# Weight decoding with its scratch in another place, and combined weights through diagonal weights, ahead of a two-layer loop

## The chip, the cores and the metric

One core of one Trainium2 chip runs the kernel. The metric is the device time of one execution in microseconds. The kernel before took 1108.55 us as the median of three runs (1108.22 to 1109.36).

## What is computed

Agent attention over 12480 tokens of 128 channels and 49 agents, and then two feed-forward layers (128 to 2048 to 128), all in float32; the weights of the layers arrive as float64, 8 bytes each:

```
a2k     = softmax(agents @ k.T * scale)        # 49 x 12480
agent_v = a2k @ v                              # 49 x 128
q2a     = softmax(q @ agents.T * scale)        # 12480 x 49
x       = q2a @ agent_v                        # 12480 x 128
x       = silu(x @ w_in) @ w_out
out     = (h * cos(h)) @ w2_out,  h = x @ w2_in
```

## The kernel before, in words

The kernel never forms x of the attention. It multiplies agent_v with w_in once ("combined weights", 49 rows of 2048) and feeds the probabilities q2a of the tokens straight to the first layer. TensorE works on numbers rounded to its float32r form; to keep precision each operand is held as a high part and the rest, a low part, and a product is taken as high x high, low x high and high x low.

It has two stages. The **first stage**, up to about 130 us, loads and prepares everything, and its order of instructions on each engine is planned ahead of time by a scheduler from dependencies and priorities. The **second stage** is the loop over 25 tiles of tokens with four groups each (lines 589 to 865); its order is written out by hand in a block of manual schedule, and the diff leaves that order as it is. The loop's buffers take the memory of the first stage's buffers, and its PSUM banks those of the first stage, so it waits for them to come free.

In the first stage tokens come in 13 blocks: twelve of 1024 tokens and one of 192. All loads are issued by the SP queue, in order. A loop over the key blocks turns them (T, lines 316 to 328), takes scores and a running maximum (k_scores). Three query steps and six decoding steps are put between. Then a loop of query steps runs: each takes a query block through turning (L323, copied by ScalarE at L327), scores (L337), maximum and difference (L119, L123), exponential (L124), normalising on GpSimd (L133), splitting into a packed tile pk of 128 columns (L145 to L147) and turning back (L156), from where a copy (L161, on ScalarE) writes the probabilities pT. Each of these is one step behind the one before. Beside them the key scores become exponentials (L383, with their sums in zk), are turned (L394, L396) and multiplied with v (L408), summing into pav over all blocks.

**Decoding.** The 8-byte weights come in 16 pieces of 128 x 512, four each of i1 (w_in), o1, i2 and o2. load_piece (L239, L241) loads one into a raw buffer wraw, of which there are three. split_a decodes: ScalarE takes the absolute value of the upper words into m (L260); VectorE shifts it into a (L264), adds the sign from the upper words (L267), takes the exponent into m (L270), and makes the rest r from the lower words and m (L273), the last reader of the raw words. split_b, one step later, finishes it: ScalarE casts a to the high half (L283), GpSimd takes a minus high half into m (L284) and adds r to give the low half (L285). a, r and m have two buffers each. Decoding has a priority 150 instructions below its place in the program.

**Combining.** After the last v block the two halves of pav go into `halves` (L478) with the reduced zk as one more column (L479); a product with `both` adds the halves (L481), then come add, reciprocal and scaling (L483 to L485), and a product with `eye3` (L487), 49 x 256, which lays the agents' rows two and a half times side by side: 128 columns for the main weights, and 19 remaining rows in four bands of 32 for the part kept apart. The result is split into avh and avl (L490, L491). Then twice, each behind a query step, four banks of products with w2h and w2l (L495 to L497):

```
for j, cast in ((0, nc.vector.tensor_copy), (2, nc.scalar.copy)):
    q_step(t)
    combine(j, cast)
    q_step_end(t)
    t += 1
```

In combine, six products give the part apart, cast (L502) and subtracted in four bands (L505) into w3; six more give the main part, which replaces w2h and w2l in place (L511 to L513). The loop's first instruction of TensorE, L610, multiplies with w3 into a PSUM pair, and L622 with w2h.

Of the kernel before, what the change touches and what calls it, by code (L numbers as in the profile page):

```python
# [8 lines left out]
F32 = mybir.dt.float32  # L9
# [26 lines left out]
def agent_attention_moe_moe_kernel(ctx, tc, q, k, v, agents, w_in, w_out, w2_in, w2_out, out):  # L36
    nc = tc.nc
# [21 lines left out]
    eye3 = const.tile([NA, 256], F32, name="eye3")  # L59
# [108 lines left out]
    with ExitStack() as att:  # L168
        raw_p = att.enter_context(tc.tile_pool(name="raw", bufs=NRAW))
        wraw_p = att.enter_context(tc.tile_pool(name="wraw", bufs=3))  # L170
        dec_p = att.enter_context(tc.tile_pool(name="dec", bufs=2))
# [61 lines left out]
        def load_piece():  # L233
# [3 lines left out]
            t = wraw_p.tile([128, 512], I64, tag="w", name="wraw")  # L237
# [9 lines left out]
        def split_a():  # L247
# [7 lines left out]
            hi, lo = (x[:, 4 * j:4 * j + 4, :].rearrange("p c d -> p (c d)") for x in split[nm])  # L255
# [5 lines left out]
            half_split.append((hi, lo, a, r, m))  # L261
# [16 lines left out]
        def split_b():  # L278
            if not half_split:
                return  # L280
            hi, lo, a, r, m = half_split.pop(0)
# [10 lines left out]
        for a in (0, NA, 2 * NA):  # L292
            n = min(NA, 128 - a)
            nc.vector.tensor_copy(out=eye3[:, a:a + n], in_=ident[:NA, :n])
        nc.vector.memset(eye3[:, 128:256], 0.0)
        for a in range(128, 256, 32):
            nc.vector.tensor_copy(out=eye3[:, a:a + REST], in_=ident[:NA, MORE:NA])
# [65 lines left out]
        both = one_p.tile([128, NA], F32, name="both")  # L363
        nc.vector.tensor_tensor(out=both, in0=ident[:, 0:NA], in1=ident[:, 64:64 + NA], op=ALU.add)
# [107 lines left out]
        halves = one_p.tile([128, C + 1], F32, name="halves")  # L472
        nc.gpsimd.memset(halves, 0.0)
        assert not todo and not raws

        avn = ag
        for x in (0, 64):
            nc.vector.tensor_copy(out=halves[x:x + NA, 0:C], in_=pav[x:x + NA])  # L478
        nc.vector.tensor_reduce(out=halves[:, C:C + 1], in_=zk, op=ALU.add, axis=AX.X)  # L479
        pav = banky("y1")[:NA, :C + 1]  # L480
        nc.tensor.matmul(out=pav, lhsT=both, rhs=halves, start=True, stop=True)  # L481
        rz = one_p.tile([NA, 1], F32, name="rz")
        nc.vector.tensor_scalar(out=rz, in0=pav[:, C:C + 1], scalar1=1e-9, scalar2=None, op0=ALU.add)  # L483
        nc.vector.reciprocal(out=rz, in_=rz)
        nc.vector.tensor_scalar(out=avn, in0=pav[:, 0:C], scalar1=rz, scalar2=None, op0=ALU.mult)  # L485
        pn = bank1()[:, :256]
        nc.tensor.matmul(out=pn, lhsT=avn, rhs=eye3, start=True, stop=True)  # L487

        avh, avl = (eT_p.tile([128, 512], F32R, tag="eT", name=nm)[:, :256] for nm in ("avh", "avl"))
        nc.vector.tensor_copy(out=avh, in_=pn)  # L490
# [24 lines left out]
        def combine(j, cast):  # L515
            pair = bank2()
            for x in range(2):
                av_times_w(pair[:, x, :], j + x, True)
            apart(pair, j, cast)
            pair = bank2()  # L520
            for x in range(2):
                av_times_w(pair[:, x, :], j + x, False)
# [347 lines left out]
```

## Time and profile before

| | |
|---|---|
| median of three runs | 1108.55 us |
| profiled execution | 1108.43 us |
| its span, first to last instruction | 1106.6 us |
| TensorE busy | 1074.5 us (97%) |
| VectorE busy | 962.3 us (87%) |
| ScalarE busy | 924.6 us (84%) |
| GpSimd busy | 541.1 us (49%) |
| mean granted clock of TensorE | 0.989 of full |

In the profile PE is TensorE, PEld its loading of weights, DVE VectorE, ACT ScalarE, POOL GpSimd and SP the engine that issues the DMAs. Busy time of PE is that of pipelined matmuls, so 97% is not 97% of its peak. A row of the timeline has the start and the length in us, the engine, the line of the kernel, the operation, the output and input tiles, the shape, the count, and in brackets how long the engine stood idle before it and what released it. Clock is the share of full speed that TensorE was granted: 1.00 is 2.4 GHz, 0.50 is 1.2 GHz, and a value between is a mix of the two over the stretch. The span includes both stages; averages over it hide that the first has other limits than the second.

### The profile page before, as it was taken

The page shows a single profiled execution, that of the slowest core. Times are in us where ns is not written, and L with a number is a line of the kernel's source. Part 1 is how long each engine was busy: PE and PEld are TensorE (multiplying, and loading weights), DVE is VectorE, ACT ScalarE, POOL GpSimd, SP SyncE. Part 2 cuts the span into 40 slices and gives each one's busy share as a digit, 9 for nine tenths or more (in the row PEclk, how much of TensorE's full clock was granted, in tenths as well). Part 3 has the DMA queues.
Part 4 walks back from the last instruction along what each step waited for, and adds up shares of the span by engine and source line. Part 5 has one row for each costly group of instructions (what it writes and reads, how often), then busy time and mean ns, then how long its engine had stood idle before and what let it go on. Part 6 is the DMA issues. An engine that isn't in the chain of part 4 may idle for free.

```text
span 1106.6 us, 14122 instructions
## 1 busy us (share of the span) xinstructions
PE 1074.5 (97%) x5227; PEld 844.5 (76%) x5227; DVE 962.3 (87%) x1023; ACT 924.6 (84%) x1005; POOL 541.1 (49%) x281
## 2 busy tenths in 40 slices
PE   8798799999999999999999999999999999999997
PEld 5597567777777777777777777777777777788996
DVE  5868469999999999999999989999999999989897
ACT  6796698888888888888888888888888888888876
POOL 2668305444455444555444555444554444555455
PEclk9998799999999999999999999999999999999999
DMA  9763000000000000000000000000000000000000
GB/s 345 285 235 139 11 6 6 14 3 15 16 8 9 16 13 4 16 16 1 16 16 11 6 16 15 1 16 16 9 8 16 13 4 15 15 5 10 10 9 16
DMA packets 66221, 38.68 MB, mean 35 GB/s; under 512 B 52523, under 2 KB 57184, under 8 KB 66152
## 3 DMA queue, kind: packets, MB, share of 16 engines
q1 hardware_dynamic: 66152, 37.78, 11.3%
q8 instruction: 41, 0.67, 0.3%
q14 instruction: 28, 0.23, 0.1%
HBM read 27.58 MB, written 6.39 MB: 31 GB/s over the span
## 4 chain that ended last, share of the span: by engine, by line
PE 87%; DVE 4%; ACT 3%; POOL 3%; DMA 2%; issue 1%; SPq 0%; POOLq 0%; DVEq 0%; ACTq 0%
PE y L654 16%; PE y L658 16%; PE y L655 16%; PE h L622 10%; PE h L696 8%; PE h L698 8%; PE h L697 8%; PE h L610 4%; DMA raw<-in_q_dram 1%; DMA wraw<-in_moe_w_in_dram 1%; POOL g2l L755 1%; DVE a L267 1%; ACT xT L327 1%; POOL m L284 1%; PE h L323 1%
## 5 line engine op out<-in xcount | busy, mean ns | idle before, releaser
L755 POOL TENSOR_TENSOR g2l<-g,g2h 128x1024 fp32r<-128x1024 f32 (+2 forms) x200 | 465.5, 2350 | 504.8 <-DVE g1l L645 495.0
L720 DVE SCALAR_TENSOR_TENSOR n<-n,h 128x1024 f32<-128x1024 int32 (+3 forms) x202 | 238.9, 1184 | 65.3 <-ACT n L710 52.1
L710 ACT ACTIVATE n<-h,quarter 128x1024 int32<-128x1024 f32 (+3 forms) x202 | 219.7, 1088 | 89.4 <-PE h L698 89.3
L645 DVE TENSOR_TENSOR g1l<-g,g1h 128x1024 fp32r<-128x1024 f32 (+2 forms) x200 | 239.6, 1198 | 23.4 <-ACT g1h L637 16.2
L737 DVE TENSOR_TENSOR g<-n,h 128x1024 f32<-128x1024 f32 (+3 forms) x202 | 237.9, 1178 | 3.4 <-ACT n L729 0.2
L630 ACT ACTIVATE g<-h 128x1024 f32<-128x1024 f32 (+2 forms) x200 | 199.5, 998 | 37.1 <-PE h L622 37.0
L729 ACT ACTIVATE n<-n,halfpi 128x1024 f32<-128x1024 f32 (+3 forms) x202 | 225.7, 1120 | 0.8 <-DVE n L720 0.8
L637 ACT CAST g1h<-g 128x1024 fp32r<-128x1024 f32 (+2 forms) x200 | 204.8, 1024 | 3.3
L746 DVE CAST g2h<-g 128x1024 fp32r<-128x1024 f32 (+2 forms) x196 | 154.5, 788 | 7.5
L654 PE MATMUL y<-g1h,o1h 128*128 128x512 f32 (+2 forms) x400 | 156.7, 392 | 0.5 <-DVE x2l L683 0.4
L654 PE MATMUL y<-g2h,o2h 128*128 128x512 f32 (+2 forms) x400 | 154.6, 386 | 1.1 <-DVE o L777 0.9
L696 PE MATMUL h<-x2h,i2h 128*128 128x512 f32 (+2 forms) x400 | 154.1, 385 | 1.0 <-DVE g L737 0.9
L655 PE MATMUL y<-g2h,o2l 128*128 128x512 f32 (+2 forms) x400 | 154.4, 386 | 0.0
L655 PE MATMUL y<-g1h,o1l 128*128 128x512 f32 (+2 forms) x400 | 154.2, 386 | 0.0
L698 PE MATMUL h<-x2l,i2h 128*128 128x512 f32 (+2 forms) x400 | 153.7, 384 | 0.0
L697 PE MATMUL h<-x2h,i2l 128*128 128x512 f32 (+2 forms) x400 | 153.7, 384 | 0.0
L622 PE MATMUL h<-pT,w2h 128*128 128x512 f32 (+2 forms) x400 | 134.5, 418 | 0.0
L658 PE MATMUL y<-g2l,o2h 128*128 128x512 f32 (+2 forms) x400 | 122.2, 386 | 1.9 <-POOL g2l L755 1.9
L658 PE MATMUL y<-g1l,o1h 128*128 128x512 f32 (+2 forms) x400 | 121.6, 385 | 0.0
L654 PEld LDWEIGHTS y<-g1h,o1h 128*128 128x128 f32 x400 | 75.5, 189 | 21.9 <-DVE x2l L683 8.3
L622 PEld LDWEIGHTS h<-pT,w2h 128*128 128x128 f32 x400 | 68.1, 190 | 31.4 <-issue 24.4
L658 PEld LDWEIGHTS y<-g2l,o2h 128*128 128x128 f32 x400 | 74.8, 188 | 17.7 <-POOL g2l L755 3.1
(119 smaller groups left out, 1145.9 us busy)
## 6 DMA issues: line engine op xcount, KB each, us to landing
raw<-in_q_dram SPq DMA_DIRECT2D x12, 512.0 KB
vraw<-in_v_dram SPq DMA_DIRECT2D x12, 512.0 KB
raw<-in_k_dram SPq DMA_DIRECT2D x11, 512.0 KB
out_dram<-o SPq DMA_DIRECT2D x88, 64.0 KB
wraw<-in_moe_w_in_dram SPq DMA_DIRECT2D x8, 512.0 KB
wraw<-in_moe_w_out_dram SPq DMA_DIRECT2D x8, 512.0 KB
x<-pT SPq DMA_DIRECT2D x88, 38.0 KB
raw<-in_k_dram SPq DMA_DIRECT2D x2, 256.0 KB
```

Source lines behind the costliest of these rows:

```text
L622: nc.tensor.matmul(out=h1s[g, k][:, j, :toks(t)], lhsT=w2h[:, 128 * c:128 * c + 128], rhs=x, start=False, stop=True)
L645: i = v.tensor_tensor(out=gl, in0=f, in1=b32(gh), op=ALU.subtract)
L654: nc.tensor.matmul(out=y, lhsT=wh[:, c, :], rhs=gh[:, j, :], start=(c == 0), stop=False)
L655: nc.tensor.matmul(out=y, lhsT=wl[:, c, :], rhs=gh[:, j, :], start=False, stop=False)
L658: nc.tensor.matmul(out=y, lhsT=wh[:, c, :], rhs=gl[:, j, :], start=False, stop=(c == NCH - 1))
L696: nc.tensor.matmul(out=y, lhsT=i2h[:, c, :], rhs=xh, start=True, stop=False)
L697: nc.tensor.matmul(out=y, lhsT=i2l[:, c, :], rhs=xh, start=False, stop=False)
L698: nc.tensor.matmul(out=y, lhsT=i2h[:, c, :], rhs=xl, start=False, stop=True)
L720: v.scalar_tensor_tensor(out=b32(n)[:, p], in0=n[:, p], scalar=-2.0 * PI, in1=h2s[g, k][:, p], op0=ALU.mult, op1=ALU.add)
L729: sc.activation(out=r[:, p], in_=r[:, p], func=AF.Sin, bias=halfpi)
L737: v.tensor_tensor(out=f[:, p], in0=r[:, p], in1=h[:, p], op=ALU.mult)
L755: i = (v if (g, k) == (NG - 1, 1) else gp).tensor_tensor(out=gl[:, p], in0=f[:, p], in1=b32(gh)[:, p], op=ALU.subtract)
```

## The change

There are two parts. In the **decoding** the raw words of o1, i2 and o2 are loaded into the very place that the two halves will take, and only i1 still uses raw buffers, two in place of three. m comes from a pool of its own, with two buffers, and is no longer written by GpSimd; the difference goes into a. a and r have three buffers. The high half of a piece now overwrites its raw words, so it is written after r has read them. In the **combining** the sum of zk goes through a product of its own, its reciprocal scales the diagonal `eye3` (now 128 x 160), one product with the unscaled `halves` gives what two gave, and the part apart is made by twelve products into one bank, with stationary tiles `spread` that are zero outside 32 columns. Both rounds of combining stand behind one query step. In combine itself only the six products per pair, the in-place casts and the subtraction remain.

```diff
-    eye3 = const.tile([NA, 256], F32, name="eye3")
+    eye3 = const.tile([128, 160], F32, name="eye3")
...
-    split = {"i1": tuple(x.rearrange("p (c d) -> p c d", d=128) for x in (w2h, w2l))}
-    for nm in ("o1", "i2", "o2"):
-        split[nm] = (
-            wts.tile([128, NCH, 128], F32R, name=f"{nm}h"),
-            wts.tile([128, NCH, 128], F32R, name=f"{nm}l"),
-        )
+    parted = {}
+
+    def halves_of(nm, j):
+
+        if nm == "i1":
+            return [x[:, 512 * j:512 * j + 512] for x in (w2h, w2l)]
+        parted[nm, j] = wts.tile([128, 2, 512], F32R, tag=f"{nm}{j}", name=nm)
+        return [parted[nm, j][:, x, :] for x in range(2)]
+
+    def part(nm, x, c):
+        return parted[nm, c // 4][:, x, c % 4 * 128:c % 4 * 128 + 128]
...
-        wraw_p = att.enter_context(tc.tile_pool(name="wraw", bufs=3))
-        dec_p = att.enter_context(tc.tile_pool(name="dec", bufs=2))
+        wraw_p = att.enter_context(tc.tile_pool(name="wraw", bufs=2))
+        dec_p = att.enter_context(tc.tile_pool(name="dec", bufs=3))
+        mag_p = att.enter_context(tc.tile_pool(name="mag", bufs=2))
...
             nm, j = to_load.pop(0)
-            t = wraw_p.tile([128, 512], I64, tag="w", name="wraw")
+            if nm == "i1":
+                t = wraw_p.tile([128, 512], I64, tag="w", name="wraw")
+            else:
+                t = wts.tile([128, 512], I64, tag=f"{nm}{j}", name="wraw")
...
-            m = dec_p.tile([128, 512], F32, tag="m", name="m")
+            m = mag_p.tile([128, 512], F32, tag="m", name="m")
...
+            nm, j, a, r = half_split.pop(0)
+            hi, lo = halves_of(nm, j)
+            f = a.bitcast(F32)
             with tc.high_priority(offset=-LATER):
-                nc.scalar.copy(out=hi, in_=a.bitcast(F32))
-                nc.gpsimd.tensor_tensor(out=m, in0=a.bitcast(F32), in1=b32(hi), op=ALU.subtract)
-                nc.gpsimd.tensor_tensor(out=lo, in0=r, in1=m, op=ALU.add)
+                nc.scalar.copy(out=hi, in_=f)
+                nc.gpsimd.tensor_tensor(out=f, in0=f, in1=b32(hi), op=ALU.subtract)
+                nc.gpsimd.tensor_tensor(out=lo, in0=r, in1=f, op=ALU.add)
...
+        nc.vector.memset(eye3, 0.0)
+        for x in (0, 64):
+            for a in (0, NA, 2 * NA):
+                n = min(NA, 128 - a)
+                nc.vector.tensor_copy(out=eye3[x:x + NA, a:a + n], in_=ident[x:x + NA, x:x + n])
+            nc.vector.tensor_copy(out=eye3[x:x + NA, 128:128 + REST], in_=ident[x:x + NA, x + MORE:x + NA])
...
-        both = one_p.tile([128, NA], F32, name="both")
-        nc.vector.tensor_tensor(out=both, in0=ident[:, 0:NA], in1=ident[:, 64:64 + NA], op=ALU.add)
+        both = one_p.tile([128, 128], F32, name="both")
+        for x in (0, 64):
+            nc.vector.tensor_tensor(out=both[:, x:x + 64], in0=ident[:, 0:64], in1=ident[:, 64:128], op=ALU.add)
...
+        spread = [v_p.tile([128, 640], F32R, tag="v", name="spread") for _ in range(2)]
+        for x in spread:
+            nc.gpsimd.memset(b32(x), 0.0)
+        halves = one_p.tile([128, C], F32, name="halves")
         nc.gpsimd.memset(halves, 0.0)
...
+        rz = one_p.tile([128, 1], F32, name="rz")
+        nc.vector.tensor_reduce(out=rz, in_=zk, op=ALU.add, axis=AX.X)
+        pz = bank1()[:, 0:1]
+        nc.tensor.matmul(out=pz, lhsT=both, rhs=rz, start=True, stop=True)
+        nc.vector.tensor_scalar(out=rz, in0=pz, scalar1=1e-9, scalar2=None, op0=ALU.add)
         nc.vector.reciprocal(out=rz, in_=rz)
...
+        nc.vector.tensor_scalar(out=eye3, in0=eye3, scalar1=rz, scalar2=None, op0=ALU.mult)
+        nc.vector.tensor_copy(out=halves[0:NA], in_=pav[0:NA])
+        nc.scalar.copy(out=halves[64:64 + NA], in_=pav[64:64 + NA])
+        pn = bank1()[:, :160]
+        nc.tensor.matmul(out=pn, lhsT=halves, rhs=eye3, start=True, stop=True)
+
+        avh, avl = (eT_p.tile([128, 512], F32R, tag="eT", name=nm)[:, :128] for nm in ("avh", "avl"))
+        spread_h, spread_l = (x.rearrange("p (i d) -> p i d", d=160)[:, :, 0:32] for x in spread)
+        four = pn[:, 128:160].unsqueeze(1).to_broadcast([128, 4, 32])
+        nc.scalar.copy(out=avh, in_=pn[:, 0:128])
+        nc.scalar.copy(out=spread_h, in_=four)
+        nc.vector.tensor_tensor(out=avl, in0=pn[:, 0:128], in1=b32(avh), op=ALU.subtract)
+        nc.vector.tensor_tensor(out=spread_l, in0=four, in1=b32(spread_h), op=ALU.subtract)
+
+        def combine_apart():
+
+            pw = banky("y1")
+            y = pw.rearrange("p (c d) -> p c d", c=4)
+            wh, wl = (w.rearrange("p (c i d) -> p c i d", i=4, d=128) for w in (w2h, w2l))
             for i in range(4):
+                for x, w in ((0, wh), (0, wl), (1, wh)):
+                    nc.tensor.matmul(
+                        out=y, lhsT=spread[x][:, 128 * i:128 * i + 128], rhs=w[:, :, i, :],
+                        start=(i == 0 and w is wh and x == 0), stop=(i == 3 and x == 1),
+                    )
+            hr = eT_p.tile([128, 512], F32R, tag="eT", name="hr")
+            nc.scalar.copy(out=hr, in_=pw)
+            nc.vector.tensor_tensor(
+                out=w3.rearrange("p c d -> p (c d)"), in0=pw, in1=b32(hr), op=ALU.subtract
+            )
...
-        for j, cast in ((0, nc.vector.tensor_copy), (2, nc.scalar.copy)):
-            q_step(t)
-            combine(j, cast)
-            q_step_end(t)
-            t += 1
+        q_step(t)
+        combine_apart()
+        combine(0, nc.scalar.copy)
+        combine(2, nc.vector.tensor_copy)
+        q_step_end(t)
+        t += 1
```

The rest of the diff renames what the loop reads: `part(nm, x, c)` in place of the two whole tiles.

## Rows read from the trace of the kernel before

**Rows 1.** Windows by stage: us, each engine busy (x instructions), clock, DMA share, GB/s.

```profile
8.00:41.00 33.00, 28.79 (x185) 17.17 (x183) 23.31 (x37) 27.04 (x39) 12.58 (x11) 1.00 0.89 332
...
55.00:85.00 30.00, 28.73 (x308) 26.76 (x309) 18.09 (x33) 29.22 (x61) 20.81 (x22) 1.00 0.69 241
...
85.00:106.00 21.00, 16.32 (x152) 14.66 (x150) 18.56 (x26) 12.16 (x23) 16.14 (x15) 0.84 0.42 151
...
106.00:131.00 25.00, 17.80 (x87) 13.73 (x86) 16.22 (x34) 13.79 (x23) 13.42 (x16) 0.84 0.04 13
...
131.00:141.00 10.00, 10.00 (x30) 6.79 (x31) 3.34 (x3) 8.67 (x10) 0.00 (x0) 0.55 0.01 2
```

**Rows 2.** Timeline, 98 to 102 us: start, us, engine, line, tiles, count, [idle before].

```profile
98.84 0.67 ACT L260 ACTIVATE m<-wraw 128x512 f32<-128x512 f32 x1 [3.83 <-POOL o2l L285]
...
100.36 0.57 ACT L161 CAST pT<-y 128x512 fp32r<-128x512 f32 x1
...
101.07 1.08 PE L156 MATMUL y<-ident,pk 128*128 128x128 f32 x4 [4.18 <-ACT pT L161]
```

**Rows 3.** Windows, finer, around the gap on TensorE.

```profile
97.00:101.00 4.00, 0.00 (x0) 0.00 (x0) 3.04 (x6) 2.16 (x6) 2.26 (x3) 0.76 0.34 118
...
101.00:106.00 5.00, 4.93 (x24) 4.48 (x24) 4.30 (x7) 2.42 (x5) 4.20 (x4) 0.50 0.01 3
...
106.00:119.00 13.00, 11.22 (x64) 9.17 (x62) 9.43 (x24) 7.20 (x15) 12.23 (x13) 0.87 0.06 19
```

**Rows 4.** Timeline, 105 to 131 us: from the last L408 to the first L610.

```profile
105.45 0.67 PE L408 MATMUL y<-vraw,eT 96*49 96x128 f32 x4
...
106.95 0.29 DVE L478 COPY halves<-y 49x128 f32<-49x128 f32 x1
...
110.56 0.42 PE L481 MATMUL y<-halves,both 128*49 128x129 f32 x2
...
113.39 0.33 DVE L485 TENSOR_SCALAR ag<-y,rz 49x128 f32<-49x128 f32 x1
...
114.16 0.70 PE L487 MATMUL h<-eye,ag 49*128 49x256 f32 x2
...
114.90 0.42 DVE L490 CAST avh<-h 128x256 fp32r<-128x256 f32 x1 [0.46 <-PE h L487]
...
115.45 0.48 PE L495 MATMUL h<-w2h,avh 128*128 128x512 f32 x1
...
118.09 0.39 PE L497 MATMUL h<-w2h,avl 128*128 128x512 f32 x1
...
126.67 1.11 ACT L511 ACTIVATE w2l<-h,from 32x1024 fp32r<-32x1024 f32 x1 [1.67 <-PE h L497]
...
127.79 1.01 ACT L512 CAST w2h<-h 96x1024 fp32r<-96x1024 f32 x1
...
128.83 1.23 DVE L513 TENSOR_TENSOR w2h<-h,w2l 32x1024 fp32r<-32x1024 f32 x1 [2.06 <-ACT w2h L512]
...
130.12 0.79 PE L610 MATMUL h<-x,w 19*128 19x512 f32 x2
```

**Rows 5.** Timeline of GpSimd, first us: a memset.

```profile
0.98 0.21 POOL L473 MEMSET halves<- 128x129 f32 x1
```

**Rows 6.** Timeline: the cast of one piece on ScalarE, its r on VectorE.

```profile
99.42 0.61 ACT L283 CAST o2h<-a 128x512 fp32r<-128x512 f32 x1
...
100.97 0.68 DVE L273 SCALAR_TENSOR_TENSOR r<-wraw,m 128x512 f32<-128x512 uint32 x1
```

**Rows 7.** Waits of the SP queue, 0 to 135 us: in total, times, longest.

```profile
SPq L241 <- DVE r L273: 29.8, 8, 7.6
```

**Rows 8.** Timeline, 11 to 16 us: a weight load on SP, and the first r.

```profile
11.06 0.42 SPq L239 DMA_DIRECT2D wraw<-in_moe_w_in_dram  x1
...
15.20 0.68 DVE L273 SCALAR_TENSOR_TENSOR r<-wraw,m 128x512 f32<-128x512 uint32 x1
```

**Rows 9.** Timeline, 93 to 95 us: r beside a GpSimd product.

```profile
93.69 1.22 DVE L273 SCALAR_TENSOR_TENSOR r<-wraw,m 128x512 f32<-128x512 uint32 x1
```

More of the change, by code (lines that the diff above doesn't have):

```diff
@@ L470, in agent_attention_moe_moe_kernel @@
             t += 1
-        halves = one_p.tile([128, C + 1], F32, name="halves")
-        nc.gpsimd.memset(halves, 0.0)
[L474 to L482, printed above, removed]
@@ L483, in agent_attention_moe_moe_kernel @@
-        nc.vector.tensor_scalar(out=rz, in0=pav[:, C:C + 1], scalar1=1e-9, scalar2=None, op0=ALU.add)
-        nc.vector.reciprocal(out=rz, in_=rz)
[L485 to L490, printed above, removed]
@@ L509, in in_place @@
-        def in_place(y, cs):
-            nc.scalar.activation(out=w2l[96:128, cs], in_=y[96:128], func=AF.Identity, scale=from98[96:128])
-            nc.scalar.copy(out=w2h[0:96, cs], in_=y[0:96])
-            nc.vector.tensor_tensor(out=w2h[96:128, cs], in0=y[96:128], in1=b32(w2l)[96:128, cs], op=ALU.subtract)
-        def combine(j, cast):
+        assert not todo and not raws
+        spread = [v_p.tile([128, 640], F32R, tag="v", name="spread") for _ in range(2)]
+        for x in spread:
+            nc.gpsimd.memset(b32(x), 0.0)
@@ L516, in combine @@
+        def combine(j, copy):
             pair = bank2()
             for x in range(2):
[L518 to L522, printed above, removed]
-            in_place(pair.rearrange("p x d -> p (x d)"), slice(512 * j, 512 * j + 1024))
-        for j, cast in ((0, nc.vector.tensor_copy), (2, nc.scalar.copy)):
-            q_step(t)
-            combine(j, cast)
-            q_step_end(t)
-            t += 1
+                cs = slice(512 * (j + x), 512 * (j + x) + 512)
+                y = pair[:, x, :]
+                nc.tensor.matmul(out=y, lhsT=avh[:, 0:128], rhs=w2h[:, cs], start=True, stop=False)
+                nc.tensor.matmul(out=y, lhsT=avh[:, 0:128], rhs=w2l[:, cs], start=False, stop=False)
+                nc.tensor.matmul(out=y, lhsT=avl[:, 0:128], rhs=w2h[:, cs], start=False, stop=True)
+            y, cs = pair.rearrange("p x d -> p (x d)"), slice(512 * j, 512 * j + 1024)
+            nc.scalar.activation(out=w2l[96:128, cs], in_=y[96:128], func=AF.Identity, scale=from98[96:128])
+            copy(out=w2h[0:96, cs], in_=y[0:96])
+            nc.vector.tensor_tensor(out=w2h[96:128, cs], in0=y[96:128], in1=b32(w2l)[96:128, cs], op=ALU.subtract)
@@ L648, in L1_lo, with three @@
             g1s[g, k] = [gh, gl]
-        def three(y, wh, wl, gh, gl, c0):
+        def three(y, w, gh, gl, c0):
             for j in range(2):
                 c = c0 + j
-                nc.tensor.matmul(out=y, lhsT=wh[:, c, :], rhs=gh[:, j, :], start=(c == 0), stop=False)
-                nc.tensor.matmul(out=y, lhsT=wl[:, c, :], rhs=gh[:, j, :], start=False, stop=False)
+                nc.tensor.matmul(out=y, lhsT=part(w, 0, c), rhs=gh[:, j, :], start=(c == 0), stop=False)
+                nc.tensor.matmul(out=y, lhsT=part(w, 1, c), rhs=gh[:, j, :], start=False, stop=False)
             for j in range(2):
                 c = c0 + j
-                nc.tensor.matmul(out=y, lhsT=wh[:, c, :], rhs=gl[:, j, :], start=False, stop=(c == NCH - 1))
+                nc.tensor.matmul(out=y, lhsT=part(w, 0, c), rhs=gl[:, j, :], start=False, stop=(c == NCH - 1))
         def L1_y(g, k):
@@ L666, in L1_y @@
             gh, gl = g1s.pop((g, k))
-            three(y1s[t], o1h, o1l, gh, gl, 4 * m + 2 * k)
+            three(y1s[t], "o1", gh, gl, 4 * m + 2 * k)
         def L1_end_a(g):
@@ L695, in L2_h @@
                 y = h[:, j, :toks(t)]
-                nc.tensor.matmul(out=y, lhsT=i2h[:, c, :], rhs=xh, start=True, stop=False)
-                nc.tensor.matmul(out=y, lhsT=i2l[:, c, :], rhs=xh, start=False, stop=False)
-                nc.tensor.matmul(out=y, lhsT=i2h[:, c, :], rhs=xl, start=False, stop=True)
+                nc.tensor.matmul(out=y, lhsT=part("i2", 0, c), rhs=xh, start=True, stop=False)
+                nc.tensor.matmul(out=y, lhsT=part("i2", 1, c), rhs=xh, start=False, stop=False)
+                nc.tensor.matmul(out=y, lhsT=part("i2", 0, c), rhs=xl, start=False, stop=True)
             h2s[g, k] = h[:, :, :toks(t)]
@@ L769, in L2_y @@
             gh, gl = g2s.pop((g, k))
-            three(y2s[t], o2h, o2l, gh, gl, 4 * m + 2 * k)
+            three(y2s[t], "o2", gh, gl, 4 * m + 2 * k)
         def L2_end(g):
```

26 lines of the change are left out of this document (1 added, 25 removed).

## The prediction

> **What bounds the kernel now.** I read the windows by stage first. The steady loop, from 141 us to the end, is written out by hand and the diff does not touch its order, so the question is how early its first instruction, L610, can start. From 55 to 85 us ScalarE is busy 29.22 us of 30.00, so there ScalarE is the bound and an earlier load brings nothing. From 85 to 106 us it is busy only 12.16 of 21.00 us while no other engine is full (VectorE 18.56, GpSimd 16.14), and from 106 to 131 us again nothing is full: these two stages are bound by waits [rows 1].
>
> The timeline shows which. At 98.84 us ScalarE starts the Abs of one weight piece (L260) after 3.83 us idle, released by GpSimd's L285: the magnitude buffer m has two places and GpSimd reads and writes it to the very end of a piece. Behind it on ScalarE stands the copy of turned probabilities (L161, 100.36 us), and TensorE has waited 4.18 us for that copy at 101.07 us [rows 2]. TensorE does nothing from 97 to 101 us, and the next 5 us run at a granted clock of 0.50, the lower of the two levels [rows 3].
>
> The second wait is a chain with little beside it. The last product with v (L408) starts at 105.45 us and takes 0.67 us. Then come copies to halves (L478), a product that folds the two halves and the denominators (L481, at 110.56 us, held up behind other TensorE work), add, reciprocal, scaling, a second product and two rounding passes (L490 is the first), until the first product with the weights (L495) starts at 115.45 us. From there two rounds of twelve products, each with its evacuations, end in L513 at 128.83 us, and L610 follows at 130.12 us [rows 4]. So 9.33 us lie between the end of L408 (106.12) and 115.45, and 14.67 us between 115.45 and 130.12.
>
> **The change part by part.** The sum is made against the profiled execution's own time, 1108.43 us (a span of 1106.60 and 1.83 around it); the median of the runs is 1108.55, 0.12 above.
>
> (1) m freed by VectorE. GpSimd's difference now goes into a, which has three places instead of two, so the Abs waits only for VectorE's r of two pieces earlier. The 3.83 us on ScalarE go; what is late next is the xT copy behind it and GpSimd's own load. Gain: of TensorE's stall of 4.18 us at most all, and of its 4.93 us at half clock at most half, 2.4, together 6.6; at least nothing. GpSimd is busy 12.23 of 13.00 us from 106 to 119 [rows 3], which caps it. I take -4.5, nearer to the stall, since L408 itself needs no GpSimd result of its own step.
>
> (2) Shorter way to the first weight product. The denominators (zk) are complete before L408, so their sum, product, reciprocal and the scaling of the diagonal leave the path. What stays after L408 is one copy on each of two engines (0.29 as L478), one product, one rounding copy and the spread copy. With 0.29, about 0.4 for the product, two at up to 0.42 (L490) and a few tenths of hand-over that is some 1.7 us at least, an estimate from these rows; at most the old 9.33. The gain lies between 0 and 7.6. The old chain has 2.45 us of work in it (L478 twice, L481, L485, L487, L490) and 6.9 of waits and two steps on one column; the new one has four of its seven links, so four sevenths of the 6.9, 3.9, plus 1.7: 5.6 us, -3.7.
>
> (3) Combining. The number of products stays 24, but the part apart now lands in one bank of 512 columns, so its evacuation is one copy of 512 and one subtraction in place of two casts of 1024 and eight small subtractions. Twelve products take 118.09 less 115.45, 2.64 us for eleven starts, 0.24 each [rows 4]. From the first product: 18 x 0.24 = 4.3 us until the first pair is ready, then on ScalarE L511 1.11, L512 1.01, L511 1.11, then L513 1.23, 8.8; with hand-overs of about 0.1 and the last step to L610, 9.3. At half clock throughout, the 24 products take 10.3 and the path 12.9. So -5.4 to -1.8; I take -4.7, near the full clock, because the gap between the two rounds is what the change removes.
>
> (4) Displaced steps. One query step instead of two covers the combining, so more of the late probabilities' work falls beside the start of the steady loop, where ScalarE is busy 8.67 of 10.00 us [rows 1]. Two more copies like L161 (0.57) and a cast of about the same: +1.7; nothing if they fill gaps, 4 if TensorE's order also puts their transposes ahead of L610.
>
> (5) New memsets. Two of 128x640 on GpSimd against 0.21 for 128x129 [rows 5]: five times as long each, 2.1 together, an estimate. They can run as soon as v buffers are free or stand in GpSimd's full queue: 0 to +2.1, I take +1.0.
>
> (6) The new wait. The high half now overwrites the raw words, so ScalarE's cast (L283) waits for r, the last reader. Before, the cast at 99.42 ran ahead of the r that ends at 101.65, by 2.23 us [rows 6]. Queued behind the cast are xT, pT and exponentials, for which TensorE and VectorE wait. Twelve pieces have this wait; the last five lie where ScalarE is not full. If the program's order puts the cast later it costs nothing, if all five hold the queue 11.2. GpSimd waited for r anyway. I take +1.5.
>
> (7) Loads. The SP queue stood 29.8 us for VectorE's r before weight pieces, at most 7.6 at once [rows 7]; twelve pieces now go where they stay and need no buffer. Since 55 to 85 us is ScalarE's, this brings nothing there; earlier ScalarE has 6.0 us idle of 33.00 from 8 to 41 us [rows 1], the most it could give. Against it, i1 has two buffers in place of three: its third piece, issued at 11.06 us, must now wait for the first r, that ends at 15.88, and key and query loads stand behind it on SP: +4.8 at most [rows 8]. Between -6.0 and +4.8 I take 0: the gain has DMA at 0.89 of its time against it, the loss five raw buffers loaded ahead.
>
> (8) Clock at the start of the loop. From 131 to 141 us the clock is 0.55 and TensorE never idle, ScalarE 8.67 of 10.00 [rows 1]. At the higher level ScalarE would be the next bound: 0 to -1.3. I take -0.6.
>
> The small tiles, the changed place of the weights and the narrower diagonal cost nothing: same bytes per partition, same shapes in the loop. Sum: -4.5 - 3.7 - 4.7 + 1.7 + 1.0 + 1.5 + 0 - 0.6 = -9.3, so 1099.1 us.
>
> **A rule weighed against the rows.** The same VectorE instruction, r, takes 0.68 us at 100.97 us [rows 6] and 1.22 at 93.69, beside a GpSimd product [rows 9]. The Trainium skill, SBUF — State Buffer, section Who interferes with whom, says that a VectorE instruction with two SBUF inputs and a GpSimd instruction that reads SBUF exclude each other on a shared port pair, one blocked until the other ends. The trace agrees with it as far as those two durations go. By that rule a removed ScalarE wait would push decoding and probabilities against each other, and term (1) would vanish: the first rival.
>
> **The rivals.** *GpSimd and VectorE pace the decoding.* Term (1) gives nothing and the memsets cost in full: 1108.43 - 3.7 - 4.7 + 1.7 + 2.1 + 1.5 = 1105.3. For it: GpSimd at 12.23 of 13.00 us, r at 1.22; against it: GpSimd is idle 4.86 of 21.00 us in the stage before. Chance 0.18. *Everything comes forward*: -6.6, -6.0 of (2), -5.4, -1.3, +1.7: 1090.8. For it, nothing is full there; against it, GpSimd. Chance 0.14. *ScalarE is held by the new wait*, slower: each high-half cast that keeps its place holds ScalarE 2.23 us, and in the ScalarE-bound stretch nothing covers that. Without (6) the sum is -10.8, so it decides from five of the twelve pieces held in full; with five it gives 1108.8, or 1113.3 where term (1) is lost too, and with eight and term (1) lost 1108.43 - 6.3 + 17.8 = 1119.9. For it: in the late pieces the cast did run ahead of r. Against it: the order is planned again for the new dependency. Chance 0.09. *No change*: the program's planner puts the combining no earlier, or the start of the loop waits for the last decoding buffers, whose place it reuses: 1108.4. Chance 0.05.
>
> **How the numbers follow.** The forecast has 0.54, at 1099.1, its own range 1094 to 1104 from terms (1) to (3). Range 1090 to 1106: it takes in both rivals on the faster side and leaves out the slower one and no change. About 0.2% (2.2 us) can be told from no change, so the first rival gives 0.03 to the same. Faster 0.54 + 0.14 + 0.15 = 0.83, same 0.03 + 0.05 = 0.08, slower 0.09.
>
> **What would show it.** Right: L260 without idle time ahead of it, TensorE without the 4 us gap after 97 us, L408 of the last v block ending near 101, its distance to the first weight product 5 to 6 us, from there to L610 9 to 10, L610 near 120. Wrong: L283 with waits for L273 summing over 10 us, GpSimd full up to the first weight product, or L610 near 130.

## The result, and the profile after

The changed kernel takes 1112.96 us (median of 13 runs, 1110.24 to 1118.69) against 1108.55 before: 1.0052 times as long, 95% interval 1.0041 to 1.0063. It is slower, where the prediction said 1099.1 and faster. The profiled execution took 1114.34 us, its span is 1112.6 against 1106.6.

Windows of the changed kernel, over the stretches of [rows 1] (same columns):

```profile
8.00:41.00 33.00, 28.02 (x164) 17.14 (x165) 21.15 (x33) 24.60 (x35) 12.55 (x11) 0.92 0.98 355
55.00:85.00 30.00, 28.27 (x303) 25.73 (x302) 20.64 (x35) 27.48 (x58) 19.56 (x20) 1.00 0.68 221
85.00:106.00 21.00, 17.75 (x163) 15.85 (x161) 20.14 (x26) 14.02 (x29) 16.00 (x15) 0.92 0.30 107
106.00:131.00 25.00, 19.49 (x94) 17.02 (x94) 16.34 (x30) 13.51 (x27) 17.12 (x19) 0.73 0.04 14
131.00:141.00 10.00, 7.92 (x28) 4.81 (x28) 2.91 (x3) 6.11 (x10) 1.56 (x3) 0.69 0.01 2
```

The third row is the one to read: from 85 to 106 us VectorE, the third busy column, is busy 20.14 of 21.00 us, against 18.56 before. No engine was full there before; now one nearly is. The chain of work that ended last, followed from 60 to 118 us, points the same way: 41% of it lies in three decoding lines of VectorE, and no other line has more than 6%:

```profile
by line: DVE a L275 14.9%; DVE r L281 13.5%; DVE m L278 12.5%; issue 7.7%; ACT m L268 6.0%; ACT sT L394 5.5%; DVE a L272 5.2%; PE y L161 3.8%; PE h L347 3.3%; ACT xT L337 3.3%; PE y L419 3.3%; ACT i L293 3.0%; ACT o L293 3.0%; DVE z L135 2.
```

The timeline from the last product with v to the loop, the places of [rows 4]:

```profile
112.29 0.67 PE L419 MATMUL y<-vraw,eT 96*49 96x128 f32 x4
...
120.00 0.47 PE L492 MATMUL h<-rz,both 128*128 128x1 f32 x2
...
121.78 0.30 DVE L495 TENSOR_SCALAR eye<-eye,rz 128x160 f32<-128x160 f32 x1
...
122.54 0.44 PE L499 MATMUL h<-eye,halves 128*128 128x160 f32 x2
...
123.61 0.48 PE L531 MATMUL h<-w2h,avh 128*128 128x512 f32 x1
...
132.71 1.23 DVE L537 TENSOR_TENSOR w2h<-h,w2l 32x1024 fp32r<-32x1024 f32 x1
...
133.99 0.50 PE L622 MATMUL h<-x,w 19*128 19x512 f32 x1
```

So the 6.0 us of span come in four pieces. The last product with v ends 6.84 us later (112.96 against 106.12). From there to the first product with the weights it takes 10.65 us in place of 9.33, +1.32. The combining itself is shorter, 10.38 in place of 14.67, -4.29. After the loop's first product another 2.1 are lost. Of the 6.84, some 2 us are probably this execution's own: a key load landed late at the start, and TensorE stood for it.

```profile
8.51 0.90 PE L333 MATMUL h<-ident,raw 128*128 128x128 f32 x3 [1.82 <-DMA raw<-in_k_dram]
```

The loads issued up to there are the same in both kernels, below, the slowest decoding has no such wait and the fastest kernel has one of 1.5 us, and the medians differ by 4.4 and not 6.0. The waits of ScalarE, 0 to 135 us (in total, times, longest), show what else is new:

```profile
ACT o L293 <- DVE r L281: 9.8, 4, 3.0
ACT i L293 <- DVE r L281: 4.1, 2, 2.6
```

The cast of the high half waits 13.9 us for r, six times. The wait of the Abs for GpSimd, in which one of [rows 2] lay, is gone.

### The profile page after: what moved, and what is told of

It reads as the page before. It is cut to its first block, busy times and chain, and to the rows that moved or that the text cites. A ratio compares the mean times of both kernels' runs of the same rounds, so it can differ in the third digit from the quotient of the medians.

```text
span 1112.6 us, 14107 instructions
## 1 busy us (share of the span) xinstructions
PE 1079.5 (97%) x5227; PEld 848.8 (76%) x5227; DVE 967.6 (87%) x1017; ACT 923.6 (83%) x1007; POOL 541.1 (49%) x283
## 4 chain that ended last, share of the span: by engine, by line
PE 88%; DVE 6%; ACT 4%; issue 1%; POOL 1%; DMA 1%; SPq 0%; POOLq 0%; ACTq 0%; DVEq 0%
PE y L666 16%; PE y L667 16%; PE y L670 16%; PE h L634 10%; PE h L708 8%; PE h L710 8%; PE h L709 8%; PE h L622 4%; DVE a L275 1%; DVE r L281 1%; DVE m L278 1%; PE y L161 1%; PE h L347 1%; ACT xT L337 1%; POOL g2l L767 1%
## 5 line engine op out<-in xcount | busy, mean ns | idle before, releaser
L666 PE MATMUL y<-g1h,o 128*128 128x512 f32 (+2 forms) x400 | 156.7, 392 | 0.4 <-DVE x2l L695 0.3
L666 PE MATMUL y<-g2h,o 128*128 128x512 f32 (+2 forms) x400 | 154.5, 386 | 1.1 <-DVE o L789 0.9
L708 PE MATMUL h<-x2h,i 128*128 128x512 f32 (+2 forms) x400 | 154.2, 385 | 1.0 <-DVE g L749 0.9
L667 PE MATMUL y<-g2h,o 128*128 128x512 f32 (+2 forms) x400 | 154.4, 386 | 0.0
L667 PE MATMUL y<-g1h,o 128*128 128x512 f32 (+2 forms) x400 | 154.3, 386 | 0.0
L710 PE MATMUL h<-x2l,i 128*128 128x512 f32 (+2 forms) x400 | 153.8, 384 | 0.0
L709 PE MATMUL h<-x2h,i 128*128 128x512 f32 (+2 forms) x400 | 153.7, 384 | 0.0
L670 PE MATMUL y<-g2l,o 128*128 128x512 f32 (+2 forms) x400 | 122.3, 386 | 1.9 <-POOL g2l L767 1.9
L670 PE MATMUL y<-g1l,o 128*128 128x512 f32 (+2 forms) x400 | 121.3, 384 | 0.0
L666 PEld LDWEIGHTS y<-g1h,o 128*128 128x128 f32 x400 | 75.3, 188 | 21.8 <-DVE x2l L695 8.3
L670 PEld LDWEIGHTS y<-g2l,o 128*128 128x128 f32 x400 | 74.8, 188 | 17.7 <-POOL g2l L767 3.1
```

The costliest lines, as they stand in the source:

```text
L666: nc.tensor.matmul(out=y, lhsT=part(w, 0, c), rhs=gh[:, j, :], start=(c == 0), stop=False)
L667: nc.tensor.matmul(out=y, lhsT=part(w, 1, c), rhs=gh[:, j, :], start=False, stop=False)
L670: nc.tensor.matmul(out=y, lhsT=part(w, 0, c), rhs=gl[:, j, :], start=False, stop=(c == NCH - 1))
L708: nc.tensor.matmul(out=y, lhsT=part("i2", 0, c), rhs=xh, start=True, stop=False)
L709: nc.tensor.matmul(out=y, lhsT=part("i2", 1, c), rhs=xh, start=False, stop=False)
L710: nc.tensor.matmul(out=y, lhsT=part("i2", 0, c), rhs=xl, start=False, stop=True)
```

## The experiments

Each ratio is to the kernel before, run beside it; "distance" below is that from the first product with v to the end of the last.

### The two parts apart

**The decoding alone**: the diff without its combining, and **the combining alone**: the reverse.

> The decoding part of the change alone; the combining as before. Theory A (the cast of the high half, which now waits for r, holds ScalarE's queue and brings the last product with v 7 us later): all of that stays and the combining gives nothing back, so 1113 to 1117 us, the cast idle for r some 14 us in total, the last product with v starting near 112. Theory B (loads: the third raw piece of i1 waits for a buffer and the keys come late): also slower, 1111 to 1114, but with the first product with v late by 3 us and no further loss after it. Theory C (the combining behind one query step instead of two costs what it gains): 1107 to 1110, as before.

> The combining part alone; the decoding as before. A and B: the last product with v starts near 105.5 as before, from the first product with the combined weights to the loop's first instruction 10.4 us in place of 14.7, the start of the loop 2 us slower to get going, so 1104 to 1108 us. C: 1110 to 1114 us.

Decoding alone 1113.59 us, 1.0041 (1.0020 to 1.0062); combining alone 1108.85, 1.0006 (0.9998 to 1.0015). The decoding is the whole loss, and the combining brings nothing net: its distance from the first weight product to the loop is 10.40 us, as in the whole change, but the last product with v ends 2.25 us later (108.37; 1.50 of it arose before the first product with v), and the stretch after the loop's start costs about 2 more. Set against the prediction's terms, the decoding was forecast at -3.0 (1, 6 and 7) and measured at +5.3 us, the combining at -6.3 (2 to 5 and 8) and measured at +0.5.

### The pieces of the decoding

**m freed, raw words apart.** Before, with one edit:

```diff
-                nc.gpsimd.tensor_tensor(out=m, in0=a.bitcast(F32), in1=b32(hi), op=ALU.subtract)
-                nc.gpsimd.tensor_tensor(out=lo, in0=r, in1=m, op=ALU.add)
+                nc.gpsimd.tensor_tensor(out=f, in0=f, in1=b32(hi), op=ALU.subtract)
+                nc.gpsimd.tensor_tensor(out=lo, in0=r, in1=f, op=ALU.add)
```

> The kernel before, with one edit: GpSimd's difference goes into a in place of m, so that the Abs on ScalarE no longer waits for GpSimd; raw buffers, halves and the number of buffers as before, so the cast does not wait for r. A: ScalarE loses its 12 us of waits ahead of the Abs and gets no new wait, so 1103 to 1108 us; VectorE may wait for a instead, by up to 4 us. B and C: nothing changes in the loads or the combining, 1107 to 1110 us.

1106.50 us, 0.9985 (0.9976 to 0.9993). The last product with v starts at 102.07 us where it was 105.45:

```profile
102.07 0.43 PE L409 MATMUL y<-vraw,eT 96*49 96x128 f32 x4
```

3.6 us come forward (its end is at 102.50), and 3.57 are given back at once, since the way to the first weight product grows from 9.33 to 12.90 us. What the loop's start gains, 1.98 us (128.14 against 130.12), comes from the combining behind it, 12.74 us in place of 14.67. Freeing m has the forecast sign, and falls short of the 4.5.

**The wait alone.** The same, plus the order that the high half comes behind r:

```diff
+                tc.add_manual_dep(i.ins, last_r.pop(0).ins.name, AFTER, reason="cast after r")
```

> The kernel with m freed and the raw words apart (which took 1106.5 us), with one edit: the cast of the high half waits for r of its piece, as in the changed kernel, though nothing overwrites the raw words. Theory A (that wait on ScalarE is the loss between the first and the last product with v): that distance grows from 43.8 to 48 to 52 us, waits of the cast for r of 8 us or more, 1109 to 1114 us. Rival D (it is not the wait but VectorE, whose decoding steps run longer beside GpSimd once pieces come early into their place): the distance stays near 44 and the time within 1105 to 1108 us.

1108.23 us, 0.9999 (0.9991 to 1.0008): 1.7 us more than without the wait, a rough figure, for the two intervals just overlap. The distance is 45.91 us, between what the two theories said. Its waits:

```profile
ACT o2h L285 <- DVE r L274: 4.1, 1, 4.1
ACT w2h L285 <- DVE r L274: 2.5, 1, 2.5
```

With the wait and m freed, then, the time is that of before, and the step from here to the decoding alone (1113.59) costs 5.4 us: raw words in place and loaded early, a third buffer for a and r, one raw buffer less for i1. The buffers are tried below.

**The cast later, and on another engine.** In the whole change, split_b moved from the head of the query step to behind its decoding steps; and, in another run, the cast on GpSimd (`nc.gpsimd.tensor_copy(out=hi, in_=f)`).

> The changed kernel with the end of the decoding (cast, difference, low half) put behind the scores and the exponential of its query step in the program instead of ahead of the normalising. A: the cast's waits for r fall from 14 us to under 5 and the last product with v starts 3 to 6 us earlier, so 1105 to 1110 us. B: the loads stay as they are, 1111 to 1115 us. C: as the changed kernel, 1111 to 1115 us.

> The changed kernel with the cast of the high half on GpSimd, which waits for r anyway, so that ScalarE has no wait for r left; GpSimd gets 16 casts of some 0.7 us more. A: the last product with v 3 to 6 us earlier than in the changed kernel (112.96), 1105 to 1110 us, unless GpSimd becomes the bound. D: VectorE and GpSimd meet more often, 1112 to 1117 us.

Later: 1111.26 us, 1.0032 (1.0019 to 1.0044), with 7.6 us of waits for r in place of 13.9. That is 1.7 off, about the price of the wait, and most of the loss stays. On GpSimd: 1116.10, 1.0081 (1.0065 to 1.0097); the cast no longer holds ScalarE, but there the Abs now waits 5.4 us for r in three waits, and it is slower still. Theory A had 1105 to 1110 us for both, and theory D, VectorE and GpSimd in each other's way, 1112 to 1117 for the second. The third rival's wait is real, but less of it did not bring the loss back.

**Buffers.** The decoding alone with two buffers of a and r in place of three (`name="dec", bufs=2`), and the same with three raw buffers of i1 besides (`name="wraw", bufs=3`).

> The decoding part alone (1113.6 us) with two buffers of a and r in place of three. If the third buffer, which lets the planner decode two pieces in a row, is the cause: 1107 to 1110 us. If it is not: 1112 to 1116 us.

> As the kernel before this one, with three raw buffers for i1 as in the kernel before the change. If the third raw piece's wait for a buffer is the cause of the late start: the first product with v starts 2 to 3 us earlier than 61.5 and the time is 2 to 4 us less than that of the same kernel with two raw buffers. If it is not: the same time within 1.5 us.

1116.11 (1.0076, 1.0060 to 1.0091) and 1115.25 us (1.0063, 1.0047 to 1.0079). Neither the third scratch buffer nor i1's lost raw buffer is the cause (the first is the one without a late key load).

### The place of the decoding in VectorE's order

VectorE's timeline of the changed kernel, about 80 us:

```profile
79.01 0.43 DVE L272 TENSOR_SCALAR a<-m 128x512 uint32<-128x512 uint32 x1 [1.83 <-ACT m L268]
79.47 1.63 DVE L275 SCALAR_TENSOR_TENSOR a<-wraw,a 128x512 uint32<-128x512 uint32 x1
81.14 1.38 DVE L278 TENSOR_SCALAR m<-a 128x512 uint32<-128x512 uint32 x1
82.55 0.69 DVE L281 SCALAR_TENSOR_TENSOR r<-wraw,m 128x512 f32<-128x512 uint32 x1
83.16 0.56 DVE L124 TENSOR_REDUCE m<-h 128x8 f32<-128x392 f32 x1
```

All four decoding steps of a piece stand ahead of the maximum of the query step (L124), for which the exponentials, the turned probabilities and the next step wait. The maximum waits for no one else: there is no bracket on its row. Before the change VectorE stood idle until the scores came (L337):

```profile
78.80 0.57 DVE L119 TENSOR_REDUCE m<-h 128x8 f32<-128x392 f32 x1 [0.21 <-PE h L337]
```

Counted in the timelines of all runs, from the reciprocal before (z) to the maximum, the decoding steps ahead of the four maxima from 77 us on:

| | steps ahead of the four maxima | the maxima start at, us |
|---|---|---|
| before | 2, 1, 3, 3 | 78.80, 86.17, 95.93, 105.56 |
| changed | 4, 5, 6, 4 | 83.16, 93.46, 104.07, 115.62 |
| decoding alone | 4, 5, 6, 4 | 83.18, 93.47, 104.20, 115.19 |
| two scratch buffers | 4, 5, 7, 4 | 81.13, 91.42, 101.54, 113.25 |
| the wait alone | 2, 2, 2, 5 | 80.34, 88.61, 96.22, 108.55 |

The changed kernel has more than twice as many, and its maxima follow one another by 10.3, 10.6 and 11.6 us in place of 7.4, 9.8 and 9.6. Three edits change that order, each in its own way.

**Decoding further behind**, `LATER = 400` in place of 150, and **one decoding step moved**, in the whole change and in the decoding alone: the sixth early step goes from behind the last key block to the third query step.

```diff
-EARLY_W = (2, 4, 6, 8, 10, 12)
+EARLY_W = (2, 4, 6, 8, 10)
...
-            work = split_a() if t >= len(EARLY_Q) else []
+            work = split_a() if t >= len(EARLY_Q) - 1 else []
```

> The changed kernel with decoding given a priority 400 instructions below its place in place of 150, so that the planner puts VectorE's decoding steps further behind the scores and sums of the query steps. Theory F (raw words in place and three buffers let the planner decode two pieces in a row, and VectorE, whose order is fixed and whose decoding steps run longer than planned beside GpSimd, comes late with the query steps): the distance from the first to the last product with v falls from 51.4 to 44 to 48 us, 1106 to 1111 us. Theory A (ScalarE's wait for r): the distance stays at 49 to 52 or grows, 1112 to 1118 us.

> The changed kernel with one decoding step moved away from the end of the key loop: five early steps instead of six, and one more in the query steps. The chain for the maximum over the keys, 5.1 us in the changed kernel and 2.6 before, has VectorE decoding steps between its links. Theory E (these make the first product with v 3 us late): the chain takes 2 to 3.5 us, the first product with v starts near 59 instead of 61.5, 1109 to 1112 us. If the 3 us come from the loads: no earlier start, 1112 to 1115 us.

> The decoding part alone (1113.6 us) with five early decoding steps and one more in the query steps, the edit that took the changed kernel from 1112.96 to 1108.1 us. If that gain came from the decoding's place in the plan: 1107 to 1110 us here too. If it came from the combining: 1112 to 1115 us.

Further behind: 1112.50 us, 1.0040 (1.0027 to 1.0054), no gain, though 0, 5, 4 and 6 steps stand ahead; theory F's 1106 to 1111 us failed here. The decoding then comes late itself: the last low half is ready only at 129.46 us instead of 119.62. One step moved: 1108.09 in the whole change (1.0001, 0.9992 to 1.0010), 1107.93 in the decoding alone (1.0001, 0.9992 to 1.0009): 4.9 and 5.7 us back. The first of the two was meant to clear the chain of the key maximum. That chain kept its decoding steps and its length, so this is not how it helped. What changed is the order later on: 3, 2, 6 and 5 steps in both runs, the first two maxima with 5 ahead of them in place of 9. The maxima come at 80.25, 87.28, 97.20 and 107.12 us in the whole change, and the distance is 44.53 and 43.13 us, against 51.44 and 51.56.

**Loads held as before.** The decoding alone, but each weight load waits until r of the piece three before is written, which is what three raw buffers enforced:

```diff
+            n = len(known) - 1 + (3 if known is last_r else 0)
+            if 3 <= n < len(loads) and n - 3 < len(last_r):
+                tc.add_manual_dep(loads[n].ins, last_r[n - 3].ins.name, AFTER, reason="as with three raw buffers")
```

> The decoding part alone (1113.6 us) with each weight load held until r of the piece three before it, as the raw buffers held it before the change; the rest as in the decoding part. If the earlier loads (on their way together with keys, queries and v) are the cause: 1107 to 1110 us. If it is the wait for r and the plan that comes with it: 1112 to 1116 us.

1107.67 us, 1.0002 (0.9993 to 1.0010): 5.9 back, with 37.2 us of waits on the SP queue for r in two rows, where the changed kernel has 6.0:

```profile
SPq L256 <- DVE r L290: 20.5, 5, 7.9
SPq L258 <- DVE r L290: 16.7, 5, 5.8
```

And VectorE's order in it, where the changed kernel had the piece first:

```profile
77.79 0.57 DVE L124 TENSOR_REDUCE m<-h 128x8 f32<-128x392 f32 x1 [1.16 <-PE h L356]
78.46 0.57 DVE L128 TENSOR_TENSOR e<-h,m 128x392 f32<-128x392 f32 x1
79.06 1.03 DVE L281 TENSOR_SCALAR a<-m 128x512 uint32<-128x512 uint32 x1
80.13 1.65 DVE L284 SCALAR_TENSOR_TENSOR a<-wraw,a 128x512 uint32<-128x512 uint32 x1
```

Now the maximum waits 1.16 us for its scores, and the piece comes behind it; 2, 2, 2 and 5 steps stand ahead of the four maxima. The cast still waits for r here, 7.3 us in three waits, without harm. Early loads as such need not cost time: the runs with one step moved keep thirteen of sixteen as early, and the last goes out at 75.21 us in place of 70.89. The cast's wait is in all three. What the three recovered runs share is fewer decoding steps ahead of the first two late maxima, 4 to 5 in place of 9. VectorE's busy share does not tell them apart: with held loads it is 19.67 of 21.00 us from 85 to 106 us, nearly as full as in the changed kernel. It is what it does first that changes.

The number of steps ahead is a rough sign, since the run with decoding further behind has 5 ahead of its first two maxima as well. Sharper is how long a block's scores lie ready before VectorE takes their maximum. The third block of the four, in the changed kernel and with decoding further behind:

```profile
97.92 1.96 PE L347 MATMUL h<-agT,xT 128*128 128x98 f32 x16
104.07 0.55 DVE L124 TENSOR_REDUCE m<-h 128x8 f32<-128x392 f32 x1
...
92.84 1.96 PE L347 MATMUL h<-agT,xT 128*128 128x98 f32 x16
99.85 0.55 DVE L124 TENSOR_REDUCE m<-h 128x8 f32<-128x392 f32 x1
```

The scores lie ready for 4.19 and 5.05 us. Summed over the first three of the four, it is 2.6 us before, 6.2 in the changed kernel, 6.4 in the decoding alone, 6.8 and 6.5 with the buffers changed, 5.7 further behind and 6.1 with the cast later, but 3.0 and 2.4 with one step moved and 1.4 with held loads. Over all twenty kernels of this document, those of 1110.7 us and more have 5.5 to 6.8, those of 1108.9 and less 1.0 to 4.8. This is a sign that goes with the loss in one profiled execution of each, not an experiment on it.

### The denominators, and both parts again

In the changed kernel the sum of zk (L490) is done at 89.88 us, but its product (L492) runs only at 120.00. It takes one of the PSUM banks (where TensorE's products land) through which the scores of the query steps turn, and its place in the program is behind the last of them.

**Denominators one query step earlier**, in the whole change; then on the combining with m freed (raw words apart), first without and then with this step; then the combined block ahead of its query step as well (`q_step(t)` moved behind `combine(2, ...)`).

> The changed kernel with the denominators' sum, product, reciprocal and the scaling of the diagonal moved one query step earlier in the program. Theory G (the denominators were not off the path: their product takes a place in the ring of two PSUM banks behind the last scores, and so comes after the last product with v): the distance from there to the first product with the combined weights falls from 10.65 to 6 to 9 us, 1108 to 1112 us. Rival H (that distance is set by GpSimd's queue, which holds up the turning on TensorE): it stays at 10 or more, 1111 to 1115 us.

> The combining part together with m freed and the raw words apart, so without the wait for r and without pieces loaded into their place. If the two parts add up: 1104 to 1107 us, with the loop's first instruction near 124 and 2 us lost after it. If the short chain now starts as soon as the last product with v is done (102.5 and 9 us after it): 1101 to 1104 us. A and D say the same here.

> The kernel with m freed, the raw words apart and the new combining (1107.25 us), with the denominators one query step earlier. G: the distance of 11.5 us falls to 7 to 9, 1103 to 1106 us. H: it stays, 1106 to 1108 us.

> As the kernel before this one, and the combining put ahead of its query step in the program instead of behind it. G and H: if the query step's work on GpSimd held the combining, the loop's first instruction comes 3 to 6 us earlier than 126.4 and 1102 to 1106 us; part is given back after it, where the query step now falls. If nothing held it there, 1105 to 1108 us.

In the whole change: 1110.71 us (1.0027, 1.0015 to 1.0040), 2.3 off. The rows of that run:

```profile
98.56 0.28 PE L469 MATMUL h<-rz,both 128*128 128x1 f32 x2
...
117.73 0.48 PE L520 MATMUL y<-w2h,spread 128*128 128x512 f32 x1
```

From the end of the last product with v (111.18) to the second row, here the first product with the weights, are 6.55 us in place of 10.65. With m freed and raw words apart: 1107.25 (0.9989, 0.9979 to 0.9999), with the denominators early 1104.72 (0.9973, 0.9963 to 0.9983), with the block ahead too 1104.23 (0.9962, 0.9950 to 0.9975).

**The change with the loads held** and the denominators early, and the same with the block ahead:

> The changed kernel whole, with the weight loads held as before (each until r of the piece three before is written) and with the denominators' product one query step earlier. If the early loads make the loss, through the order of the decode steps that they let in (decoding alone gave it back when held: 1107.7 against 1113.6), and the denominators add their 2.3 us: 1103 to 1107 us, the last product with v by 107 us. If holding the loads helped only by the chance of another order, and combining brings the loss back: 1108 to 1112 us, the last product with v after 109 us.

> The same, with a combined block issued ahead of the query step beside it. If the effects add, another 0.5 us less (as between the two runs with a raw buffer apart, 1104.7 and 1104.2): 1102 to 1106 us, and it stands level with the best so far or beats it. If the cast's wait for r, which this kernel keeps and the best so far hasn't, costs what it cost alone (1.7 us): 1104.5 to 1107 us.

1104.03 us, 0.9969 (0.9958 to 0.9981), and 1102.22, 0.9947 (0.9933 to 0.9960). The effects add: held loads give 6.7 in the whole change as well (1110.71 to 1104.03), and the last run beats both kernels. Its first weight product and first loop product come at 112.35 and 125.30 us, against 115.45 and 130.12 before:

```profile
112.35 0.77 PE L544 MATMUL h<-w2h,avh 128*128 128x512 f32 x1
...
125.30 0.80 PE L635 MATMUL h<-x,w 19*128 19x512 f32 x4
```

## Why the prediction was wrong

**The step that failed is (7), the loads at 0.** It weighed the transfers (SP's wait, the DMA share) and said that "twelve pieces now go where they stay and need no buffer"; the loads were bounded between -6.0 and +4.8. It missed what else the buffer did: it paced the decoding. With the raw words in place early, the plan put whole pieces of VectorE's decoding ahead of the query step's maximum. Held loads, or one step elsewhere, give back 4.9 to 6.7 us by the medians and 4.3 to 6.4 by the ratios, so the term was some +5, about at its upper bound and by another mechanism. That holding the loads gives the loss back is shown, by one edit in the decoding alone and again in the whole change; that it does so through VectorE's order is the reading that fits the rows. Step (2) failed by nearly as much, 5.0 us, see below.

The premise of (7) that 55 to 85 us is ScalarE's, so that an earlier load brings nothing there, did not hold to its end. In the kernel before, the chain of work passes from 70.83 to 84.12 us through two query loads with one turning between them, and TensorE stood for both, if only for 0.24 and 0.63 us:

```profile
76.81 1.09 PE L323 MATMUL h<-ident,raw 128*128 128x128 f32 x8 [0.24 <-DMA raw<-in_q_dram]
84.17 1.09 PE L323 MATMUL h<-ident,raw 128*128 128x128 f32 x8 [0.63 <-DMA raw<-in_q_dram]
```

In the changed kernel no load is in the chain from 60 to 118 us; VectorE's decoding has taken that place.

(1) m freed, -4.5: the Abs wait went, as said, and the last product with v came 3.6 us forward with raw words apart. But the time fell by only about 1.7 (0.9985 of 1108.31), for the query steps' scores and turnings on TensorE came ahead of the halves' product (107.48 us, behind 102.50). Mis-sized: the step did not ask what is late next after L408.

(2) The shorter way, -3.7 with 5.6 us left: it measured +1.3 with 10.65 left. The argument that zk is "complete before L408", so that its product leaves the path, failed. The operand was ready, the place in TensorE's order was not. This term missed by 5.0 us, and moving the place alone gave 2.3 of time back. With that place put right the way is 6.55 us (6.86 in the best run with raw words apart), near the 5.6.

(3) Combining, -4.7: measured -4.29, and 10.40 us alone. Right in size. (4) Displaced steps, +1.7: +2.1 after the loop's start, about 2 in the combining alone. Right in size; no run tried it by itself. (8) The clock from 131 to 141 us is 0.69 in place of 0.55, but TensorE is busy only 7.92 of 10.00 us there, so its share can't be read apart.

(5) Memsets, +1.0: they take 0.63 us each, not 1.05, so 1.26 in place of 2.1 on GpSimd; what they cost in time was not tried.

```profile
100.16 0.63 POOL L486 MEMSET spread<- 128x640 f32 x1
```

(6) The cast's wait, +1.5: six waits of 13.9 us in all. Alone, 6.6 us of waits cost 1.7, and 6.3 us less of them in the whole change gave 1.7 back; what all 13.9 cost was not measured. The size fits what was tested.

Of the rivals, the third had the side and nearly the number: held "with term (1) lost too" it gave 1113.3. Its mechanism is there, six casts of 2.3 us each, but the runs that tried it moved the time by 1.7, and the three recovered runs keep 6.1 to 7.3 us of such waits. That its number is near is luck. The first, GpSimd and VectorE pacing the decoding, named the engine that became full, at 1105.3, on the faster side (its sum leaves out term 8; with it, 1104.7). In the changed kernel r takes 0.69 us at 82.55 and 1.64 beside GpSimd's difference (L294, 91.54 us, 1.45):

```profile
91.90 1.64 DVE L281 SCALAR_TENSOR_TENSOR r<-wraw,m 128x512 f32<-128x512 uint32 x1
```

The Trainium skill, SBUF — State Buffer, section Who interferes with whom, says that such pairs exclude one another; the durations agree with it. But by VectorE's groups its sixteen pieces take 59.4 us in the changed kernel and 57.7 in the decoding with held loads, against 53.2 before. In the two runs with one step moved they take 56.6, with two scratch buffers, the slowest decoding of all (1116.11), 57.0, and with m freed (1106.50) 55.9. A lengthening that is as large in a recovered run as in the slowest one does not separate them. How much it costs by itself stays open: no run changed the durations and kept the order, and with the cast on GpSimd the forecast of rival D did come true. That the order is the cause rests on three runs that changed it by two different edits and got the loss back, while buffers and the cast's place did not, and on how long the scores lay ready. The count of steps is no law: the run with decoding further behind has 5 on its first two maxima as well, and the one with the cast later 1 and 4, and both stay slow. Why the planner chose this order was not followed further, and an order written out by hand with early loads was not tried.

## What to carry to other kernels

A buffer that makes a load wait may be what paces its readers: where an order is planned ahead, ask what a removed wait lets run early, and ahead of which step of the chain it will land on a shared engine. A work item whose operands are ready still has to get its place in the engine's order and its PSUM bank; read where it will stand, not when it could start. A gain in one stretch is counted only after naming what is late next.

## What was not expected

The SP queue's waits for r were 42.8 us before in two rows (29.8 in [rows 7], 13.0 for the other line) and 6.0 after, and the kernel without them is slower; put back by hand in the whole change they are worth 6.7 us. The length of a wait says little about its price: 6.6 us of cast waits, tried alone, cost about 1.7, and moving the cast to GpSimd, where it waits 1.2 us for r, costs 3.1 more. A last product with v that ends 14 us earlier (99.10 with held loads, 113.09 without) brought the loop's start only 6.7 us forward (129.37 against 136.11).
